# Expert rows loaded and transposed as two half-width tiles in place of two tiles of 128 rows

## Chip, cores and metric

The kernel runs on one core of one Trainium2 chip. The metric is the device time of one execution in microseconds (us), and three executions of the kernel before are given. One further execution was taken with the hardware profiler, and every duration below that comes from a trace is from that one.

## What is computed

The reference does three things in a row, all in float32:

- attention within clusters: 2 batches, 8 heads, 768 positions, head size 64; a query attends to the keys whose nearest of 16 centroids is its own;
- a mixture of 8 experts on the 1536 resulting rows of 512 numbers: every row goes to the one expert that its logits pick;
- a bilinear layer on all rows, 512 to 1536 to 512.

The part that this case is about is the second:

```python
for e in range(E):
    mask = expert_idx == e
    h = np.maximum(x[mask] @ w1[e], 0.0)
    out[mask] = gate_w[mask, None] * (h @ w2[e])
```

## The kernel before

**Rows.** While attention runs, each finished row of `x` is written by an indirect DMA to a table `xs_d` in device memory, in which every expert has a region of its own. An expert's rows therefore lie one behind another, from the start of its region.

**Turns.** The experts are worked off in 8 turns, and the turn of an expert depends on how many rows it has. Turn `e` has a fixed width `WIDTHS[e]`, the number of rows that it takes: 256, 160, 256, 224, 248, 216, 192, 176. Rows that do not fit would go through a rare path (`rare`), which these inputs do not enter. A turn's kind follows from its width: over 224 rows "three", over 176 "two", else "one". The kind says how a float32 product is put together: "three" and "two" use a rounded high part and a low part of both operands (F32R), "one" multiplies plain float32.

**One turn's rows.** `load_xe(e)` reads the expert's first row number from `turn_i` into a register of ScalarE and issues one DMA on ScalarE's queue (line 1194): 256 rows of 2 KB, row `c*128 + p` to partition `p`, tile `c`. It reads 256 rows whatever the width. `trans_x(e)` turns them on TensorE (line 1213): 2 tiles times 4 blocks of 128 columns, eight transposes, the loaded block as weights and the 128x128 identity as the moving operand, into two banks of PSUM. ScalarE and VectorE copy the first `WIDTHS[e]` columns out (lines 1218, 1222, 1224). Turn 0 gets its rows in another way (`near_load`, `near_trans`) and is not touched.

**The order around it.** Loop index `G` counts steps of 128 hidden units, 8 to a turn. A step issues `layer1(G)` (TensorE lines 1232, 1305, 1313, 1314 into `h`, then ScalarE and VectorE make `hh`), at `f == 5` of a turn the transposes for the next turn and the load for the one after, then `layer2(G - 2)` (TensorE lines 1349, 1353, 1354 into `y`), and then `split_some`, which takes weights that were loaded to a ring of four buffers `raw` (DMA on SyncE's queue, line 159), rounds them on ScalarE (line 210) and subtracts on VectorE (line 213); the subtraction frees the buffer for the next load. Each engine works its list off strictly in this order. A step's `h` and the two banks of `trans_x` come from one ring of four PSUM banks (`turn_bank`). `put_rows` writes a turn's result to `ys_d` on SyncE's queue (line 1373). The tile `xe` shares its two buffers with the results `ys`.

Of the kernel before, what the change touches and what calls it, by code (L numbers as in the profile page):

```python
# [9 lines left out]
F32 = mybir.dt.float32  # L10
# [12 lines left out]
P = 128  # L23
FAR = float(2.0 ** 100)
CAP = 256
WIDTHS = (256, 160, 256, 224, 248, 216, 192, 176)
# [25 lines left out]
def kernel(  # L52
# [15 lines left out]
    nc = tc.nc  # L68
# [14 lines left out]
    CT = CAP // P  # L83
# [16 lines left out]
    xs_d = dram.tile([NE * RX, DM], F32, name="xs_d")  # L100
# [157 lines left out]
    identr = left.tile([P, P], F32R, name="identr")  # L258
# [640 lines left out]
    for s in range(nst):  # L899
        g_, h, t = steps[s]  # L900
        pp = g_[0]
        i = s % SPP
# [6 lines left out]
        if s >= SPP and zeros:  # L909
            dst, src = zeros.pop(0)  # L910
# [150 lines left out]
    def new_x(key, dt=F32R):  # L1061
        return big.tile([P, 2, DC, CAP], dt, tag="xT", name=f"xT_{key}", bufs=2)
# [8 lines left out]
    key, cap, held, over, obase, pbase = (left.tile([P, 1, NE], F32, name=n) for n in ("key", "cap", "held", "over", "obase", "pbase"))  # L1071
# [119 lines left out]
    def load_xe(e):  # L1191
        t = big.tile([P, CT, DM], F32R, tag="xe", name=f"xe_{e}", bufs=2)
        at_row = nc.values_load(turn_i[0:1, NE + e:NE + e + 1], engines=[mybir.EngineType.Activation], min_val=RX, max_val=(NE - 1) * RX)
        i = nc.scalar.dma_start(out=t.bitcast(F32), in_=xs_d[bass.ds(at_row, CAP), :].rearrange("(c p) d -> p c d", p=P))
        if e == 1:
            for o in scatters:
                tc.add_manual_dep(i.ins, o.name, DATA, reason="rows of every scatter")
        xe_t[e] = t
# [3 lines left out]
    def turn_bank():  # L1202
        ring[0] += 1
        return ("et0", "et1", "pp", "pv")[(ring[0] - 1) % 4]

    def trans_x(key, src):

        x = new_x(key, F32 if KINDS[key] == "one" else F32R)
        hi, lo = x[:, 0], x[:, 1]
        pts = [ps_t.tile([P, 2, CAP], F32R, tag=turn_bank(), name=f"xT_{key}_{u}") for u in range(2)]  # L1210
        for t in range(CT):
            for j in range(DC):
                nc.tensor.transpose(pts[j // 2][:, j % 2, t * P:(t + 1) * P], src[:, t, j * P:(j + 1) * P], identr)
        pts = [p.bitcast(F32) for p in pts]
        wd = WIDTHS[key]
        if KINDS[key] == "one":
            for u in range(2):
                (nc.vector.tensor_copy if u else nc.scalar.copy)(hi[:, 2 * u:2 * u + 2, :wd], pts[u][:, :, :wd])
            xT_t[key] = x
            return  # L1220
        for u in range(2):
            nc.scalar.copy(hi[:, 2 * u:2 * u + 2, :wd], pts[u][:, :, :wd])
        for u in range(2):
            nc.vector.tensor_sub(lo[:, 2 * u:2 * u + 2, :wd], pts[u][:, :, :wd], hi[:, 2 * u:2 * u + 2, :wd])
        xT_t[key] = x
# [273 lines left out]
    for G in range(total_f + tot + LAG):  # L1499
# [10 lines left out]
        if I < 0:  # L1510
            layer1(G)
            if G in (2, NF - 1):
                load_xe(1 if G == 2 else 2)
            if G == NF:
                further()
            if G == GR - 2:
                tc.mark_branch_hint_location("rare", "LikelyTaken", engines=[mybir.EngineType.DVE])
            e, f = divmod(G, NF)
            if 2 * NF <= G < 3 * NF:
                next(rr, None)  # L1520
            if G > 3 * NF:
                next(gg, None)
            if f == (5 if e else NF - 2):
                if e + 1 < NE:
                    trans_x(e + 1, xe_t[e + 1])
            if f == 5 and 0 < e < NE - 2:
                load_xe(e + 2)
        elif I < tot:
            bil1(I)
            next(pg_, None)  # L1530
# [52 lines left out]
```

## Time and profile before

| | us |
|---|---|
| three executions | 764.43, 764.62, 766.75 |
| median | 764.62 |
| the profiled execution | 765.42 |
| its span in the trace | 763.9 |
| TensorE busy in the span | 750.4 |
| expert turns, by their instructions | about 285 to 460 |

Attention comes first, then the expert turns, then the bilinear layer, whose weights are loaded and split while the last turns run. Trace times are microseconds from the start of the span. PE is TensorE's matrix multiplications, PEld its weight loads, DVE VectorE, ACT ScalarE, POOL GpSimd, SP SyncE; a q behind an engine's name is its queue of DMA issues. "Granted clock" is the share of TensorE's full speed that the chip allowed. A DMA is carried by up to 16 DMA engines; "DMA share" is their mean busy share.

### The profile page before, as it was taken

The numbers are of one execution on the slowest core, as the hardware profiler recorded it, in microseconds if no ns is written. First come the engines' busy times: TensorE is split into PE (matmuls) and PEld (weight loads), VectorE is DVE, ScalarE is ACT, GpSimd is POOL, SyncE is SP. The second block draws the span as 40 slices with busy tenths as digits, with TensorE's granted clock in tenths as the row PEclk, the third lists the DMA queues.
The fourth block names the chain that finished last, engine by engine and source line by source line (L and its number), as shares of the span: only waits on it lengthen the run. The fifth ranks groups of instructions, "written<-read, shape, count | busy, mean of one in ns | idle before, by whom it ended". The sixth has DMA issues, their size and how long they took to land.

```text
span 763.9 us, 12711 instructions
## 1 busy us (share of the span) xinstructions
PE 750.4 (98%) x4788; PEld 629.7 (82%) x4788; DVE 464.3 (61%) x912; ACT 374.3 (49%) x770; POOL 106.3 (14%) x145
## 2 busy tenths in 40 slices
PE   8999999999999999999999999999999999999996
PEld 5767777777777679998999999888898888888995
DVE  6877676787867677478876898677643121121211
ACT  4656766777676675366655565344332121111211
POOL 6303203051300041000000004122001020000201
PEclk9999999999999999999999999999999999999999
DMA  6327133161321026889879877554401010000100
GB/s 189 84 87 252 43 95 90 59 195 58 91 52 32 28 97 231 313 283 298 285 240 279 276 220 219 121 146 111 137 7 52 1 56 0 1 1 0 56 1 28
DMA packets 47747, 91.86 MB, mean 120 GB/s; under 512 B 6264, under 2 KB 19832, under 8 KB 47680
## 3 DMA queue, kind: packets, MB, share of 16 engines
q1 hardware_dynamic: 43472, 81.01, 35.5%
q0 software_dynamic: 2304, 6.31, 2.2%
q10 hardware_dynamic: 1904, 3.67, 1.4%
q8 instruction: 39, 0.64, 0.4%
q14 instruction: 28, 0.23, 0.1%
HBM read 69.27 MB, written 14.04 MB: 109 GB/s over the span
## 4 chain that ended last, share of the span: by engine, by line
issue 28%; PE 26%; DMA 3%; DVE 1%; POOL 1%; ACT 1%; POOLq 0%; SPq 0%; ACTq 0%; DVEq 0%
PE ab L1232 7%; PE y L1349 5%; PE y L1353 3%; PE h L1313 3%; PE h L1232 2%; DMA raw<-in_moe_w_dram 2%; PE h L1305 2%; PE o_sc L1480 1%; PE h L1314 1%; PE y L1354 1%; POOL out_dram L1458 1%; DVE w L213 1%; PE o_pp L1480 1%; PE o_pv L1480 1%; ACT w L210 1%
## 5 line engine op out<-in xcount | busy, mean ns | idle before, releaser
L1436 DVE TENSOR_TENSOR ga<-ab,ga 128x256 f32<-128x256 f32 (+1 forms) x48 | 26.7, 557 | 156.7 <-PE ab L1232 110.9
L634 ACT ACTIVATE E<-sc,nmx 128x768 f32<-128x768 f32 x96 | 86.8, 904 | 53.9 <-DVE nmx L629 46.7
L1232 PE MATMUL ab<-xT_b,w 128*128 128x256 f32 (+1 forms) x720 | 113.1, 304 | 0.0
L1232 PE MATMUL ab<-x,w 128*128 128x512 f32 x432 | 108.1, 390 | 0.0
L1232 PEld LDWEIGHTS ab<-xT_b,w 128*128 128x128 f32 x720 | 98.6, 190 | 7.2
L629 DVE TENSOR_REDUCE nmx<-sc 128x1 f32<-128x768 f32 x96 | 91.4, 953 | 6.8 <-PE sc L621 5.6
L1232 PEld LDWEIGHTS ab<-x,w 128*128 128x128 f32 x432 | 81.1, 188 | 17.2
L652 PEld LDWEIGHTS et<-ident,E 128*128 128x128 f32 x576 | 62.3, 140 | 32.4 <-ACT ET L656 12.8
L1435 ACT COPY ga<-ab 128x256 f32<-128x256 f32 (+1 forms) x48 | 23.1, 481 | 126.9 <-PE ab L1232 123.7
L652 PE MATMUL et<-ident,E 128*128 128x128 f32 x576 | 82.4, 279 | 1.6 <-ACT E L634 1.2
L658 DVE COPY ET<-et 128x384 f32<-128x384 f32 x96 | 52.6, 548 | 50.5 <-PE et L652 50.3
L620 PE MATMUL sc<-K,Q 80*128 80x512 f32 x192 | 73.0, 380 | 0.0
L679 PE MATMUL pv<-ET,v 128*64 128x384 f32 (+2 forms) x408 | 72.3, 479 | 0.3 <-DVE xrow L699 0.2
L213 DVE TENSOR_TENSOR w<-raw,w 128x1024 fp32r<-128x1024 f32 x48 | 58.1, 1218 | 19.3 <-ACT w L210 18.8
L1480 PE MATMUL o_sc<-w,g 128*128 128x512 f32 x288 | 69.5, 390 | 0.0
L1437 ACT CAST g<-ga 128x256 fp32r<-128x256 f32 (+1 forms) x48 | 24.7, 514 | 84.2 <-DVE ga L1436 84.2
L1480 PEld LDWEIGHTS o_sc<-w,g 128*128 128x128 f32 x288 | 53.9, 188 | 11.3
L621 PE MATMUL sc<-K,Q 128*128 128x512 f32 x192 | 61.3, 340 | 0.0
L1349 PE MATMUL y<-hh,w 128*128 128x256 f32 (+3 forms) x416 | 59.2, 290 | 0.0
L210 ACT CAST w<-raw 128x1024 fp32r<-128x1024 f32 x47 | 49.4, 1053 | 16.3 <-DMA raw<-in_moe_w_dram 12.3
L1349 PEld LDWEIGHTS y<-hh,w 128*128 128x128 f32 x416 | 54.4, 190 | 0.3 <-DVE ys L1323 0.3
L656 ACT COPY ET<-et 128x384 f32<-128x384 f32 x96 | 45.7, 476 | 2.7 <-PE et L652 2.7
(277 smaller groups left out, 1206.9 us busy)
## 6 DMA issues: line engine op xcount, KB each, us to landing
raw<-in_moe_w_dram SPq DMA_DIRECT2D x48, 512.0 KB, 5.1
w<-in_moe_w_dram SPq DMA_DIRECT2D x16, 512.0 KB, 9.7
raw<-in_moe_w_a_dram SPq DMA_DIRECT2D x12, 512.0 KB, 5.1
raw<-in_moe_w_b_dram SPq DMA_DIRECT2D x12, 512.0 KB, 4.5
raw<-in_moe_w_out_dram SPq DMA_DIRECT2D x12, 512.0 KB, 3.6
xs_d<-zero SPq DMA_DIRECT2D x8, 512.0 KB, 6.4
xe<-xs_d ACTq DMA_DIRECT2D x7, 512.0 KB, 6.5
v<-in_v_dram SPq DMA_DIRECT2D x8, 384.0 KB, 3.1
```

The source lines that it names most:

```text
L210: (nc.scalar.copy if late is None else nc.vector.tensor_copy)(hi, w)
L213: nc.vector.tensor_sub(lo, w, hi)
L620: nc.tensor.matmul(ps[:, lo:hi], Q3[:, qs], K3[:, h * S + lo:h * S + hi], start=True, stop=False)
L621: nc.tensor.matmul(ps[:, lo:hi], Q2[:, qs], K2[:, h * S + lo:h * S + hi], start=False, stop=True)
L629: nc.vector.tensor_reduce(out=nmx[pp][:, h, t:t + 1], in_=sc[s], axis=AX.X, op=ALU.max, negate=True)
L634: nc.scalar.activation(e, sc.pop(s), AF.Exp, bias=nmx[pp][:, h, t:t + 1], accum_out=sums[pp][:, t, h:h + 1])
L652: nc.tensor.transpose(pt[:, j * P:(j + 1) * P], e[:, kt * P:(kt + 1) * P], ident)
L658: nc.vector.tensor_copy(dst, src)
L679: nc.tensor.matmul(pv[h * D:(h + 1) * D, :], vt[:, h, kt, :], ets[g, h][:, kt, :n * P], start=(kt == 0), stop=(kt == NT - 1))
L1232: nc.tensor.matmul(ps, s_, m_, start=(i == 0), stop=(i == len(ops) - 1))
L1349: nc.tensor.matmul(ys_ps[e][j // 2][:, j % 2, :wd], w[:, m_, ff, j * P:(j + 1) * P], s_, start=(f == 0 and i == 0 and j % 2 == 0), stop=(l ...
L1480: nc.tensor.matmul(o_ps[ck][t], s_[:, t * P:(t + 1) * P], w_[:, m_], start=(f == 0 and i == 0), stop=(J == I and f == NF2 - 1 and i == 2))
```

## The change

For turns 1 to 7 the rows of a turn are loaded as two tiles of `h = WIDTHS[e] // 2` rows: row `c*h + p` goes to partition `p`, tile `c`. The load takes `WIDTHS[e]` rows, not 256, and fills `h` partitions, not 128. The eight transposes take `h` rows each, and the moving operand is the identity's `h` by `h` corner. `h` is 80, 128, 112, 124, 108, 96, 88 for the turns 1 to 7. What is copied out of PSUM is the same columns as before.

```diff
     def load_xe(e):
         t = big.tile([P, CT, DM], F32R, tag="xe", name=f"xe_{e}", bufs=2)
...
-        i = nc.scalar.dma_start(out=t.bitcast(F32), in_=xs_d[bass.ds(at_row, CAP), :].rearrange("(c p) d -> p c d", p=P))
+        h = WIDTHS[e] // CT
+        i = nc.scalar.dma_start(out=t[:h].bitcast(F32), in_=xs_d[bass.ds(at_row, CT * h), :].rearrange("(c p) d -> p c d", p=h))
...
         hi, lo = x[:, 0], x[:, 1]
+        h = WIDTHS[key] // CT
         pts = [ps_t.tile([P, 2, CAP], F32R, tag=turn_bank(), name=f"xT_{key}_{u}") for u in range(2)]
         for t in range(CT):
             for j in range(DC):
-                nc.tensor.transpose(pts[j // 2][:, j % 2, t * P:(t + 1) * P], src[:, t, j * P:(j + 1) * P], identr)
+                nc.tensor.transpose(pts[j // 2][:, j % 2, t * h:(t + 1) * h], src[:h, t, j * P:(j + 1) * P], identr[:h, :h])
```

## Rows read from the trace of the kernel before

**Rows 1.** The page: engine totals, and the granted clock in 40 slices.
```profile
PE 750.4 (98%) x4788; PEld 629.7 (82%) x4788; DVE 464.3 (61%) x912; ACT 374.3 (49%) x770; POOL 106.3 (14%) x145
PEclk9999999999999999999999999999999999999999
```

**Rows 2.** Busy time by stretch in the expert turns; the first line names the columns.
```profile
core 0: us, PE busy (x) PEld busy (x) DVE busy (x) ACT busy (x) POOL busy (x), PEclk, DMA share, GB/s
335.00:350.00 15.00, 13.90 (x120) 13.70 (x118) 12.75 (x24) 9.47 (x16) 0.00 (x0) 1.00 0.90 284
350.00:360.00 10.00, 9.41 (x71) 9.24 (x72) 9.05 (x17) 7.08 (x14) 0.00 (x0) 1.00 0.86 287
360.00:440.00 80.00, 80.00 (x592) 78.69 (x591) 62.12 (x129) 48.06 (x104) 1.26 (x1) 1.00 0.85 269
```

**Rows 3.** TensorE's waits from 285 to 460, the longest: total, times, longest.
```profile
PE h L1232 <- DVE hh L1310: 1.7, 1, 1.7
```

**Rows 4.** The chain that ended last, from 320 to 352: start, length, what.
```profile
319.92 0.69 PE h L1305 x5
...
324.35 7.55 DMA raw<-in_moe_w_dram
...
334.25 5.03 DMA raw<-in_moe_w_dram
...
341.64 6.15 DMA raw<-in_moe_w_dram
```

**Rows 5.** All transposes and loads of the turns' rows: ns min/median/max, first and last start.
```profile
L1213 PE MATMUL xT<-identr,xe x56: 221/247/333, 304.9 to 431.1; 128*128 128x128 f32 x56
L1194 ACTq DMA_DIRECT2D xe<-xs_d x7: 392/392/477, 294.4 to 413.0; - x7
DMA to landing us min/median/max: 5.0/6.5/8.1
```

**Rows 6.** TensorE in order of time, around turn 1's transposes: start, length, what.
```profile
303.74 1.36 PE L1232 MATMUL h<-xT,w 128*128 128x256 f32 x10
304.94 0.80 PE L1213 MATMUL xT<-identr,xe 128*128 128x128 f32 x8
305.57 0.59 PE L1349 MATMUL y<-hh,w 128*128 128x256 f32 x3
```

**Rows 7.** TensorE from 300 to 440: the transposes of turns 3 and 4.
```profile
343.77 0.80 PE L1213 MATMUL xT<-identr,xe 128*128 128x128 f32 x8
...
367.72 0.80 PE L1213 MATMUL xT<-identr,xe 128*128 128x128 f32 x8
```

**Rows 8.** ScalarE from 318 to 440: the issues of the loads for turns 3 and 4.
```profile
324.32 0.48 ACTq L1194 DMA_DIRECT2D xe<-xs_d  x1
...
348.84 0.39 ACTq L1194 DMA_DIRECT2D xe<-xs_d  x1
```

**Rows 9.** DMA from 348.8 to 360: the loads' queue, and the issue with its landing.
```profile
q10 hardware_dynamic: 272, 0.52, 13.6%
...
xe<-xs_d ACTq DMA_DIRECT2D x1, 512.0 KB, 5.3
```

**Rows 10.** The page, the loads' queue: packets, MB, share of 16 engines' span.
```profile
q10 hardware_dynamic: 1904, 3.67, 1.4%
```

**Rows 11.** ScalarE from 352 to 360; in brackets its idle time before, and the releaser.
```profile
355.49 1.05 ACT L210 CAST w<-raw 128x1024 fp32r<-128x1024 f32 x1 [1.73 <-DMA raw<-in_moe_w_dram]
...
358.03 1.05 ACT L210 CAST w<-raw 128x1024 fp32r<-128x1024 f32 x1 [1.01 <-DMA raw<-in_moe_w_dram]
```

**Rows 12.** VectorE from 357 to 361.
```profile
358.13 0.39 DVE L1318 SCALAR_TENSOR_TENSOR hh<-hf,hh 128x224 fp32r<-128x224 f32 x1
...
360.67 0.39 DVE L1318 SCALAR_TENSOR_TENSOR hh<-hf,hh 128x224 fp32r<-128x224 f32 x1
```

**Rows 13.** TensorE from 355 to 364.
```profile
360.20 0.37 PE L1353 MATMUL y<-hh,w 128*128 128x448 f32 x1
...
362.70 0.37 PE L1353 MATMUL y<-hh,w 128*128 128x448 f32 x1
```

## The prediction

> **What bounds the kernel now.** I read the page first. TensorE is busy 750.4 of 763.9 us, and its granted clock stays at the upper level, 2.4 GHz, through all 40 slices [rows 1]. So whatever shortens TensorE's own work is worth its full time, and whatever makes it wait costs its full time, unless a wait elsewhere swallows it. I looked for such waits in the expert turns, where the change lies.
>
> The table of stretches then shows those turns more closely [rows 2]. From 360 to 440 TensorE is busy without a gap. It falls short by 1.10 us between 335 and 350 and by 0.59 us between 350 and 360, and the list of waits names this as one wait of 1.7 us, on VectorE's `hh` [rows 3]. The DMA share is 0.85 to 0.90 in these stretches: the weights stream is close to what the 16 engines carry.
>
> The chain of waits tells what is behind that one wait [rows 4]. It leaves TensorE at about 320.6 and then consists of three loads of raw weights, 7.55, 5.03 and 6.15 us to land, with a rounding on ScalarE and a subtraction on VectorE between them, until `hh` comes late. VectorE and ScalarE work in order, so a late weight load holds up an activation that stands behind it. Two conclusions follow. TensorE time saved between 320 and 350 is lost in that wait, while time saved before 319 or after 351 counts. And the stage has little room for a slower transfer.
>
> **The change, part by part: the transposes.** There are 56, eight a turn [rows 5]. Their time on the path is their pitch, not the 247 ns that one takes: the eight of turn 1 start at 304.94 and the next product at 305.57, so 0.63 / 8 = 79 ns each. The ten products of 256 columns before them take (304.94 - 303.74) / 10 = 120 ns each [rows 6]. The trace shows no such transpose with fewer than 128 columns. From these two rows a column is worth (120 - 79) / 128 = 0.32 ns, and I take that slope, as 128 columns is the nearest width shown and 80 to 124 lies just beyond it. The bounds are no gain at all (the weight load, which still has 128 columns, sets the pitch) and full proportion, 79 / 128 = 0.62 ns a column. The columns saved are 128 - h: 48, 0, 16, 4, 20, 32, 40 for turns 1 to 7. Turn 3's transposes run at 343.8 [rows 7], inside the part whose gain the wait at 350 swallows. That leaves 144 columns times 8 transposes: 1152 x 0.32 = 0.37 us gained, between 0 and 1152 x 0.62 = 0.71. Nothing is removed in number: the same eight weight loads, the same semaphores, the same copies out of PSUM.
>
> **The loads get smaller.** All seven together shrink from 7 x 256 = 1792 to 1472 rows of 2 KB. None is late today: they land after 5.0 to 8.1 us, and the first is issued 304.9 - 294.4 = 10.5 us before its transposes, the last 18 us before [rows 5]. So an earlier landing is worth nothing in itself, and what can count is room for the weights stream beside it. One load takes 13.6% of 16 engines over 11.2 us, which is 1.52 us of every engine, or 95 ns for each of its 16 packets there [rows 9]. Turn 3's load is issued at 324.3, beside the 7.55 us load of the chain [rows 4, 8]. It drops from 16 to 14 packets an engine: 2 x 95 ns = 0.19 us, at most, off the wait at 350. I count 0.18, with 0 to 0.2 as its ends. Turn 1's load shrinks most, 6 x 95 = 0.57 us of every engine, but it runs at 294 [rows 5], before the chain leaves TensorE at 320.6, so I count nothing; if that cover were gone it would be 0.57.
>
> **The loads may get less even.** Today's loads fill 128 partitions and left 1904 packets on their queue, 272 each: 256 of data and 16 more, one for each engine [rows 10]. So each of the 16 engines has had an equal share of 16 rows. 80, 112 and 96 partitions can be cut into 16 equal shares too. 124 (turn 4), 108 (turn 5) and 88 (turn 7) cannot. No row shows what the chip does then. It could give some engines one partition more than others, and nothing would be lost. Or it could keep the shares equal and use fewer engines: 124 = 4 x 31, so 4 engines; 108 = 12 x 9, so 12; 88 = 11 x 8, so 11. Since all seven loads shown have equal shares, I take the second as likelier. Turn 5 would then have 18 packets on 12 engines, 2 x 95 ns more, and turn 7 its old 16 on 11 engines; both are too small to count. Turn 4 would have 62 packets on each of 4 engines, 62 x 95 = 5.9 us of work in place of 1.52: those four engines get 4.4 us more to do.
>
> The Trainium skill speaks on this point, in "DMA: Bandwidth & Descriptors", section "Why a DMA increments its semaphore by 16 and not by 1": the number of engines for one transfer is the largest number up to 16 that divides the slowest dimension of both sides, with 100 partitions on 10 engines as its example. By that rule turn 4 would run on 4 engines and the sum be the one below; without it the first rival's. No run here shows the rule yet, apart from 128 partitions on 16.
>
> **What those 4.4 us cost.** The load itself stays covered: even at half speed beside the weights, 62 packets end about 12 us after the issue at 348.8, near 361, and its transposes are at 367.7 [rows 7, 8]. But every weight load needs all 16 engines to land, so the stream is as late as its slowest four. The engines have 14% idle between 350 and 360 [rows 2], 1.4 us that the four can use to catch up: the stream falls 4.4 - 1.4 = 3.0 us behind. Just there ScalarE already waits for the weights, 1.73 us before the rounding at 355.49 and 1.01 us before that at 358.03 [rows 11], so ScalarE and VectorE take the delay over in full. TensorE does not at once: `hh` is written by 358.52 and first read by `y` at 360.20, the next by 361.06 and read at 362.70 [rows 12, 13], a slack of 1.7 us. TensorE would wait 3.0 - 1.7 = 1.3 us. The ends are 0, if the stream catches up as it goes, and 4.4 - 1.7 = 2.7 if the 14% are gaps that the four engines cannot use. Behind 360 no weight load is waited for that long again and TensorE has no gap until 440, so what is lost there stays lost.
>
> **The sum.** -0.37 (transposes) - 0.18 (chain at 350) + 1.3 (turn 4's load) = +0.75 us. Against the profiled execution's own 765.42 us that is 766.2; the median of the three is 0.80 below the profiled one, so the forecast for the median is 764.62 + 0.75 = 765.4. Its own range, from the ends: -0.71 - 0.2 + 0 = -0.9 to 0 + 0 + 2.7 = +2.7, which is 763.7 to 767.3. A measurement of this kernel can tell about 0.3%, 2.3 us, from no change, so this is no change.
>
> **Rivals.** First, the 124 rows are spread over all 16 engines, or the lag of four is caught up in time. Then only the two gains stand: -0.55, between -0.9 and 0, or 764.1. For it speaks that the load's landing has 6 us to spare and that the stream refills behind 360; against it that ScalarE has no cover at 355 to 358 [rows 11].
>
> Second, and slower: turn 4's load holds back the ring of four `raw` buffers at 350 to 360 by the full 4.4 us, and TensorE finds no slack, because the late activations also hold the PSUM banks that the next `h` needs, earlier than `y` reads them. Then +4.4 - 0.55 = +3.85, or 768.5. It decides against "no change" from a wait of 2.3 + 0.55 = 2.85 us on. For it speaks that the wait at 350 today is of just that kind, an `h` that waits for an `hh` [rows 3]; against it the 1.7 us of slack in the rows that follow.
>
> Third, faster: with less traffic beside it, the chain of three loads lands so much earlier that the wait of 1.68 us at 350 is gone, and the transposes gain in full proportion: -1.68 - 0.71 = -2.4, or 762.2. Against it speaks that only 0.19 us of engine time is taken from beside that chain.
>
> **Chances.** Forecast 0.55, first rival 0.26, second 0.13, third 0.06. The range for 8 in 10 covers the forecast and the first rival with their bounds, and a little for the scatter of the three executions: 763.0 to 767.6. Faster by over 0.3% needs the third rival: 0.06. Slower by over 0.3% needs the second or the forecast's upper end: 0.14. The rest, 0.80, is no change.
>
> **What would show it.** The transposes' pitch in the changed trace: 79 ns at h = 128, 64 ns at h = 80 if the slope of 0.32 holds. Turn 4's load: its time to landing, about 12 us in place of 5.3, and completions on its queue fewer than 16 would show 4 engines. ScalarE's waits for raw weights from 350 to 362: some 3 us more in the forecast, the same as now in the first rival. A new wait of TensorE between 358 and 368, about 1.3 us, shows the forecast's main term; none there shows the first rival; 3 us or more the second. I would be wrong altogether if a difference appeared in attention or in the bilinear layer, where the change touches nothing.

## The result, and the profile after

The changed kernel takes 771.84 us (median of six, 770.92 to 776.44) against 764.52 us for the kernel before on the same chip: a ratio of 1.0098, with an interval of 1.0078 to 1.0118. It is 7.3 us slower, above the end of the forecast's range at 767.6. Its profiled execution took 773.53 us, with a span of 772.0 us, against 765.42 and 763.9 before.

I take the views in the order in which the forecast took them. First the page of the changed kernel: TensorE's total and the queue of the rows' loads (packets, MB, share of the engines' span).

```profile
PE 753.3 (98%) x4788; PEld 631.5 (82%) x4788; DVE 464.6 (60%) x912; ACT 374.4 (48%) x770; POOL 106.2 (14%) x145
...
q10 hardware_dynamic: 1563, 3.02, 1.3%
```

TensorE has as many instructions as before and is busy 2.9 us longer [rows 1], so part of the loss is work that got slower. The queue's packets are 1472 of data, as the change has it, and 91 others, where 16 a load would be 112 [rows 10]. Four loads with 16, and 4, 12 and 11 for turns 4, 5 and 7, make 64 + 27 = 91.

Next, in the changed kernel, TensorE's longest waits from 285 to 470, and the table of stretches around them (columns as in [rows 2]).

```profile
PE y L1355 <- DVE hh L1320: 4.9, 1, 4.9
PE h L1234 <- DVE hh L1312: 1.1, 1, 1.1
```

```profile
core 0: us, PE busy (x) PEld busy (x) DVE busy (x) ACT busy (x) POOL busy (x), PEclk, DMA share, GB/s
...
355.00:360.00 5.00, 5.00 (x39) 4.90 (x38) 2.21 (x3) 0.00 (x0) 0.00 (x0) 1.00 0.96 237
360.00:365.00 5.00, 1.23 (x8) 0.91 (x7) 0.93 (x1) 1.54 (x3) 0.00 (x0) 0.84 0.56 153
365.00:370.00 5.00, 3.83 (x12) 3.34 (x13) 4.13 (x9) 4.56 (x9) 0.00 (x0) 0.50 0.59 196
370.00:375.00 5.00, 5.00 (x33) 4.79 (x32) 4.78 (x12) 3.36 (x7) 0.00 (x0) 0.97 0.80 268
```

The old wait at 350 is still there, a little shorter (1.1 against 1.7 us, [rows 3]). A new one of 4.9 us stands in turn 3's products, where [rows 2] had no gap. From 365 to 370 the granted clock is 0.50, the lower level of 1.2 GHz: TensorE has just waited and now computes at half speed. The DMA share tells the rest: 0.96 from 355 to 360, then 0.56. The engines were nearly all busy first; what a few of them still did afterwards is shown below.

The chain of waits (start, length, what) in the changed kernel names the transfer:

```profile
325.47 8.25 DMA raw<-in_moe_w_dram
...
343.44 5.21 DMA raw<-in_moe_w_dram
...
351.09 11.89 DMA raw<-in_moe_w_dram
363.00 1.05 ACT w L210
...
365.63 0.40 DVE hh L1320
366.17 0.71 PE y L1355
```

A raw weight load takes 11.89 us where its like before had landed by the cast at 355.49 [rows 11]. Rounding, subtraction (left out of the lines above) and `hh` follow it without a gap, and the product starts the moment `hh` is there. ScalarE's order of time has the load's issue and what the weights cost (idle time in brackets):

```profile
349.71 0.53 ACTq L1195 DMA_DIRECT2D xe<-xs_d  x1
...
353.52 1.05 ACT L210 CAST w<-raw 128x1024 fp32r<-128x1024 f32 x1 [0.21 <-DMA raw<-in_moe_w_dram]
...
363.00 1.04 ACT L210 CAST w<-raw 128x1024 fp32r<-128x1024 f32 x1 [8.15 <-DMA raw<-in_moe_w_dram]
...
365.44 1.05 ACT L210 CAST w<-raw 128x1024 fp32r<-128x1024 f32 x1 [0.91 <-DMA raw<-in_moe_w_dram]
```

Turn 4's load is issued at 349.71. In the packet records its data runs from 352.85 to 364.65, so the weight load, issued at 351.09, lands 1.7 us before the uneven load is through. The DMA view from 352.8 to 364.8 has the mean busy share in tenths, in 40 slices of 0.3 us, and the load's queue:

```profile
DMA  3699999895889999987989999999965333222222
...
q10 hardware_dynamic: 252, 0.51, 17.4%
```

From 362.1 on the share is 0.2 to 0.3, where four busy engines of 16 would make 0.25. The weight load's completions, one for each engine, tell the same: twelve came by 356.74, the other four at 360.12, 360.13, 362.96 and 362.97.

Last, TensorE's order of time in the changed kernel: turn 1's transposes, and the products about the wait.

```profile
306.07 0.77 PE L1215 MATMUL xT<-identr,xe 80*128 80x80 f32 x8
306.66 1.70 PE L1351 MATMUL y<-hh,w 128*128 128x256 f32 x12
...
360.97 0.26 PE L1316 MATMUL h<-xT,w 128*128 128x224 f32 x1
366.17 0.71 PE L1355 MATMUL y<-hh,w 128*128 128x448 f32 x1 [4.94 <-DVE hh L1320]
366.68 0.39 PE L1356 MATMUL y<-hh,w 128*128 128x224 f32 x1
...
375.77 0.79 PE L1215 MATMUL xT<-identr,xe 124*128 124x124 f32 x8
```

The starts of each turn's transposes make a ledger of where the time goes (us from the start of the span; the last column is the span):

| | turn 1 | 2 | 3 | 4 | 5 | 6 | 7 | span |
|---|---|---|---|---|---|---|---|---|
| before | 304.94 | 322.50 | 343.77 | 367.72 | 389.56 | 410.97 | 430.51 | 763.9 |
| after | 306.07 | 323.62 | 344.89 | 375.77 | 397.70 | 419.11 | 438.65 | 772.0 |
| later by | 1.13 | 1.12 | 1.12 | 8.05 | 8.14 | 8.14 | 8.14 | 8.1 |

Everything that the change costs comes between turn 3's transposes and turn 4's: 8.05 - 1.12 = 6.93 us. The 1.13 us were there before the first changed instruction: turn 1's load is issued at 295.55, where before it was at 294.42 [rows 5]. In kernels of the experiments that lose no time turn 1's transposes start up to 1.20 us later than before, so I don't count the 1.13 as the change's. The 6.93 consist of three parts. The wait near 350 ends at 351.45 (350.58 before), 0.87 later, which is 0.25 less than turn 3's 1.12. The first product behind the new wait starts at 366.17 (360.20 before, [rows 13]), 5.97 later, so this part adds 5.10. The last is the stretch from there to turn 4's transposes: 375.77 - 366.17 = 9.60 us where before the same work took 367.72 - 360.20 = 7.52, 2.08 us more at the lower clock.

### The profile page after: what moved, and what is told of

Its sections match the earlier page's. It is cut to its first block, busy times and chain, and to the rows that moved or that the text cites. A ratio compares the mean times of both kernels' runs of the same rounds, so it can differ in the third digit from the quotient of the medians.

```text
span 772.0 us, 12709 instructions
## 1 busy us (share of the span) xinstructions
PE 753.3 (98%) x4788; PEld 631.5 (82%) x4788; DVE 464.6 (60%) x912; ACT 374.4 (48%) x770; POOL 106.2 (14%) x145
## 3 DMA queue, kind: packets, MB, share of 16 engines
q10 hardware_dynamic: 1563, 3.02, 1.3%
## 4 chain that ended last, share of the span: by engine, by line
issue 28%; PE 25%; DMA 4%; DVE 2%; POOL 1%; ACT 1%; POOLq 0%; SPq 0%; ACTq 0%; DVEq 0%
PE ab L1234 6%; PE y L1351 4%; DMA raw<-in_moe_w_dram 3%; PE y L1355 3%; PE h L1315 2%; PE h L1234 2%; PE h L1307 2%; PE o_sc L1482 1%; PE y L1356 1%; DVE w L213 1%; PE h L1316 1%; POOL out_dram L1460 1%; PE o_pp L1482 1%; PE o_pv L1482 1%; ACT w L210 1%
```

## The experiments

The theory after the result: turn 4's 124 partitions go to 4 of the 16 DMA engines, the weight loads behind them wait for those four, and TensorE waits for the weights. Rivals: the smaller transposes or the smaller loads themselves, the uneven loads of turns 5 and 7, or the clock as the main cost. Differences of time below are against the kernel before in the same set of runs, whose median was 765.36 us for the first four kernels, 764.13 for the next four and 764.35 for the last four.

**Even loads, all else changed.** The same rows go to the same places, but each load fills all 128 partitions, so that tiles overlap in rows that nothing reads.

```diff
-        i = nc.scalar.dma_start(out=t[:h].bitcast(F32), in_=xs_d[bass.ds(at_row, CT * h), :].rearrange("(c p) d -> p c d", p=h))
+        r = P
+        rows = xs_d[bass.ds(at_row, CAP), :].rearrange("(c p) d -> p c d", p=P)
+        (sp, _), (_, nc_), (sd, nd) = rows.ap
+        rows = dataclasses.replace(rows, ap=((sp, r), (h * sp, nc_), (sd, nd)))
+        i = nc.scalar.dma_start(out=t[:r].bitcast(F32), in_=rows)
...
```

> The changed kernel, but every load of turns 1 to 7 fills all 128 partitions again (row c*h + p to partition p, for p up to 127; partitions h and up hold rows that nobody uses). The transposes stay h rows wide. If the 124-partition load on few DMA engines is the cause: no wait of TensorE over 2 us between 350 and 380, no fall of the granted clock there, and the time back at that of the kernel before, 764.5 within 1.5 us. If the transposes of h rows, or the halves as such, are the cause: the time stays near 771.8.

Measured: 765.04 us, ratio 0.9997 (0.9981 to 1.0013). TensorE's longest waits from 285 to 470, and the stretch in which the changed kernel stood still:

```profile
PE h L1239 <- issue: 0.8, 1, 0.8
PE h L1239 <- DVE hh L1317: 0.4, 1, 0.4
```

```profile
360.00:370.00 10.00, 10.00 (x69) 9.57 (x68) 9.53 (x23) 7.20 (x15) 0.00 (x0) 1.00 0.98 268
```

With even loads the long wait and the low clock are gone, and so is the whole loss. The transposes, which are as in the changed kernel, are free of it, and they bring no gain either.

**Only turn 4 changed.** The other turns are as before; the same edit stands where the transposes set `h`.

```diff
-        h = WIDTHS[e] // CT
+        h = WIDTHS[e] // CT if e == 4 else P
```

> The kernel before, with turn 4 alone (width 248, h = 124) loaded and transposed in the new way. If turn 4's load is the whole cause: about +7 us, 771 to 772.5, with the long wait of TensorE near 361 to 366. If the seven turns share the loss, or code placement does it: well under half of that, 765 to 767.5.

Measured: 771.98 us, ratio 1.0081 (1.0049 to 1.0112). The longest wait, and the stretch:

```profile
PE y L1355 <- DVE hh L1320: 3.7, 1, 3.7
```

```profile
360.00:370.00 10.00, 6.35 (x23) 5.51 (x22) 7.02 (x13) 6.95 (x15) 0.00 (x0) 0.66 0.62 182
```

The change of one turn brings the whole loss, wait and clock included.

**All turns but turn 4 changed.** The same line with `e != 4`.

```diff
-        h = WIDTHS[e] // CT
+        h = WIDTHS[e] // CT if e != 4 else P
```

> The changed kernel, with turn 4 alone loaded and transposed as before. If turn 4's load is the whole cause: 764 to 765, although turns 5 and 7 still load on 12 and 11 DMA engines. If those two cost as well: each of them shows as a later start of the transposes that follow, together over 1 us.

Measured: 765.55 us, ratio 1.0008 (0.9989 to 1.0027), with the wait at 350 as it was and no other of over 0.8 us:

```profile
PE h L1234 <- DVE hh L1312: 1.8, 1, 1.8
```

The loads of turns 5 and 7, on 12 and 11 engines, cost nothing: from turn 4's transposes to turn 7's it takes 62.78 us, and 62.79 before. Together the three runs show the place. What remains is how the 124 partitions turn into 7 us.

**Work in place of the wait.** To ask what the clock costs, a step's `h` products just ahead of the wait are computed four times, 3.8 us more of TensorE work, so that TensorE isn't idle there.

```diff
-            for j in range(DC):
+            for _ in range(4 if G == 26 else 1):
+                for j in range(DC):
...
```

> The changed kernel, in which TensorE computes h of step 26 four times in place of once, with the same result: 24 more matrix products, about 3.8 us of work, placed just ahead of the long wait at 361. If the wait ends with the late weights and costs 4.9 us, and the halved clock behind it costs another 2 us: the extra work fits in the wait, which shrinks to about 1.2 us, the clock stays at the upper level, and the time falls by about 2 us, to 769.5 to 770.5. If the clock falls for another reason or costs nothing: the time stays at 771.8, or rises by up to 3.8.

Measured: 771.78 us (768.16 to 773.11), ratio 1.0079 (1.0056 to 1.0103): the median of the changed kernel, so the gain that was expected didn't come. In its profiled execution, of 768.95 us, ScalarE's wait for the weights is 5.00 us instead of 8.15, TensorE has no long wait behind 360 and the clock stays up:

```profile
358.72 1.05 ACT L210 CAST w<-raw 128x1024 fp32r<-128x1024 f32 x1 [5.00 <-DMA raw<-in_moe_w_dram]
```

```profile
360.00:370.00 10.00, 10.00 (x66) 9.54 (x65) 8.60 (x17) 7.66 (x17) 0.00 (x0) 1.00 0.71 228
```

That execution is one of the two quickest of ten, and here the weights were late by less, so it can't stand for the median. What the run shows is that 3.8 us of extra work cost nothing in the median, as if it fitted into the wait. The clock's own share of the median stays open.

**Loads rounded up to 16 partitions.** As the first experiment, with `r` the next multiple of 16 above `h`; the loads are smaller than before and still even.

```diff
-        r = P
+        r = min(-(-h // 16) * 16, P)
```

> The changed kernel, but each load fills the number of partitions rounded up to a multiple of 16: 80, 128, 112, 128, 112, 96, 96 for turns 1 to 7 (row c*h + p; the partitions past h hold rows nobody uses). Still fewer rows than before. If only the count of DMA engines matters: as the kernel before, 764 to 765.5, perhaps 0.2 us faster by the smaller loads. If a smaller load helps the weights stream beside it by itself: 1 us or more faster.

Measured: 765.06 us, ratio 1.0009 (0.9994 to 1.0023). The queue (1504 packets of data and 7 x 16):

```profile
q10 hardware_dynamic: 1616, 3.08, 1.3%
```

There are 288 fewer data packets than before and no gain can be measured: the traffic that the change saves is worth nothing that shows here.

**Four engines in later turns.** Is it the place or the shape? Turn 4's load is made even, and turns 5, 6 and 7 each fill 124 partitions. The edit is the first experiment's with another `r`.

```diff
-        r = P
+        r = {4: P, 5: 124, 6: 124, 7: 124}.get(e, h)
```

> The changed kernel with turn 4's load over 128 partitions (even), but the loads of turns 5, 6 and 7 over 124 partitions each, so 62 packets on each of 4 engines three times. If a load on four engines costs wherever it is: three times 5 us, 775 to 780. If it costs only where the rounding on ScalarE already waits for weights, as at 350 to 358: under 2 us in all, 764.5 to 766.5.

Measured: 770.92 us, ratio 1.0092 (1.0064 to 1.0121), between the two expectations. By the starts of the transposes the three loads cost 0.09 us (turns 4 to 5), 2.05 (5 to 6) and 3.18 (6 to 7), all different. Another 1.3 us are lost behind turn 7's transposes, where the granted clock is 0.66 from 435 to 440. The two longest waits:

```profile
PE xT L1220 <- DMA xe<-xs_d: 3.0, 1, 3.0
PE y L1360 <- DVE hh L1325: 1.8, 1, 1.8
```

The second is the weights' wait, in turn 5. The first is new: turn 7's transposes wait for their own load. So a load on four engines can also be late itself, and what it costs depends on the place, from nothing to over 4 us.

**Half of the load on four engines.** Turn 4's tile 0 fills 124 partitions and its tile 1 all 128: the four engines carry 31 + 8 = 39 packets, the others 8.

```diff
-            i = nc.scalar.dma_start(out=t[:h].bitcast(F32), in_=xs_d[bass.ds(at_row, CT * h), :].rearrange("(c p) d -> p c d", p=h))
+            nc.scalar.dma_start(out=t[:h, 0].bitcast(F32), in_=xs_d[bass.ds(at_row, h), :])
+            rows = xs_d[bass.ds(at_row, CAP), :].rearrange("(c p) d -> p c d", p=P)[:, 0]
+            i = nc.scalar.dma_start(out=t[:, 1].bitcast(F32), in_=dataclasses.replace(rows, offset=rows.offset + h * DM))
```

> The changed kernel, with turn 4's load as two: tile 0 over 124 partitions (31 packets on each of 4 engines), tile 1 over 128 (8 packets on each of 16). So the four engines carry 39 packets in place of 62. If the delay of the weights goes with the packets beyond an even share (23 in place of 46): half the delay, about 3.3 us, less the slack of 1.7: a wait near 1.6 us, and 766 to 767.5. If any use of four engines is enough: 770 to 772.

Measured: 767.04 us, ratio 1.0034 (1.0019 to 1.0049), as expected of a cost that grows with the packets of the busiest engines, though the wait is half of the 1.6 us expected. The wait and ScalarE's wait for the weights:

```profile
PE y L1361 <- DVE hh L1326: 0.8, 1, 0.8
```

```profile
358.89 1.05 ACT L211 CAST w<-raw 128x1024 fp32r<-128x1024 f32 x1 [4.02 <-DMA raw<-in_moe_w_dram]
```

**Two engines.** The other direction: two loads of 62 partitions, 2 x 31, for turn 4. The queue has 1563 packets again, with 2 + 2 completions in place of 4. The second part's completions come 11 us after the first's, as they would behind it on the same two engines, which then carry 124 packets each.

```diff
-        i = nc.scalar.dma_start(out=t[:h].bitcast(F32), in_=xs_d[bass.ds(at_row, CT * h), :].rearrange("(c p) d -> p c d", p=h))
+        rows = xs_d[bass.ds(at_row, CT * h), :].rearrange("(c p) d -> p c d", p=h)
+        for a, b in (((0, 62), (62, h)) if e == 4 else ((0, h),)):
+            i = nc.scalar.dma_start(out=t[a:b].bitcast(F32), in_=rows[a:b])
```

> The changed kernel, with turn 4's load as two of 62 partitions each, which are 2 x 31: if the engines are the largest number up to 16 that divides the partitions, both run on two engines, with 62 completions in all fewer than sixteen each, and 124 packets on each of those two. The lag then doubles, 108 packets beyond an even share: about 15 us of delay for the weights, a wait of 12 us or more, and the load itself, some 24 us to land, late for its transposes: 780 to 790. If the chip spreads 62 partitions over more engines: 771 or less.

Measured: 770.19 us, ratio 1.0079 (1.0055 to 1.0104): no worse than four engines, against the expectation. ScalarE's waits for the weights are spread over more loads, and TensorE's longest wait is shorter:

```profile
359.12 1.04 ACT L210 CAST w<-raw 128x1024 fp32r<-128x1024 f32 x1 [5.24 <-DMA raw<-in_moe_w_dram]
361.98 1.05 ACT L210 CAST w<-raw 128x1024 fp32r<-128x1024 f32 x1 [1.33 <-DMA raw<-in_moe_w_dram]
365.10 1.05 ACT L210 CAST w<-raw 128x1024 fp32r<-128x1024 f32 x1 [0.61 <-DMA raw<-in_moe_w_dram]
```

```profile
PE y L1357 <- DVE hh L1322: 2.8, 1, 2.8
```

The load drained in 20.8 us, and the weight loads behind it took 9.75, 9.4 and 11.06 us to land. So no weight load waited for the end of this load, and in the changed kernel the first one didn't either (362.97 against 364.65): they are late, but not by the whole of what the uneven load still has to move.

**The changed kernel, a second execution.**

> The changed kernel once more, for a second trace of it. If the long wait is fixed by the packets of turn 4's load: again 4.9 us within 0.3, with the weight load behind it 11.9 us to land. If it hangs on how the two transfers meet: another wait, between 2 and 6 us, since the two other traces with 62 packets on four engines showed 3.7 us, and one that 3.8 us of other work covered.

Measured: 774.77 us in one execution, too few for a verdict on the time. The new wait is 3.1 us, with another of 0.8 behind it and 1.8 at 350, and the granted clock falls twice, to 0.75 from 350 to 355 and to 0.62 from 365 to 370. The weight loads issued while turn 4's load runs, before (350.2 to 356.5) and here (350.5 to 356); the last number is the median time to landing:

```profile
raw<-in_moe_w_dram SPq DMA_DIRECT2D x4, 512.0 KB, 5.1
```

```profile
raw<-in_moe_w_dram SPq DMA_DIRECT2D x3, 512.0 KB, 11.2
```

The median is 6.1 us later; the first weight load behind turn 4's takes 11.53 us, 6.3 more than before, near the 6.6 of the first trace. How the delay splits into waits and slow work differs between executions: from turn 3's transposes to turn 4's it takes 8.9 us more than before here, 6.9 in the first trace.

**Turn 4's load on SyncE's queue**, the one that the weights use, so that the uneven load stands ahead of the weights behind it. The read of its first row number moves to SyncE with it (a line left out below).

```diff
...
-        i = nc.scalar.dma_start(out=t[:h].bitcast(F32), in_=xs_d[bass.ds(at_row, CT * h), :].rearrange("(c p) d -> p c d", p=h))
+        i = (nc.sync if e == 4 else nc.scalar).dma_start(out=t[:h].bitcast(F32), in_=xs_d[bass.ds(at_row, CT * h), :].rearrange("(c p) d -> p c d", p=h))
```

> The changed kernel, with turn 4's load issued on SyncE's queue, the one that the weights use, in place of ScalarE's. The same 62 packets on four engines, but now strictly ahead of the next weight load in one queue. If the excess is the packets alone: the next weight load lands about 4.4 us late, after some 9.7 us, TensorE waits 2 to 3 us, and the time is 767 to 769. If two queues that share four engines make no difference either way: 771 to 772.

Measured: 772.35 us, ratio 1.011 (1.0087 to 1.0134): far from the first expectation and 0.35 us above the second, that the queue makes no difference. The same row, from 350.2 to 356, and the longest wait:

```profile
raw<-in_moe_w_dram SPq DMA_DIRECT2D x4, 512.0 KB, 11.8
```

```profile
PE y L1355 <- ACT ys L1364: 6.4, 1, 6.4
```

With the load ahead of them on their own queue the weights take 11.8 us. From ScalarE's queue the changed kernel's load delays them as much, 11.2 and 11.9 in its two traces. No difference shows here between the two queues.

**Seven and five engines.** Turn 4's load in two parts of 119 = 7 x 17 and 5 partitions: 34 packets on two engines, 36 on five, if the second part uses five of the seven. The edit is against the kernel of the two engines.

```diff
-        for a, b in (((0, 62), (62, h)) if e == 4 else ((0, h),)):
+        for a, b in (((0, 119), (119, h)) if e == 4 else ((0, h),)):
```

> The changed kernel, with turn 4's load as 119 partitions (7 x 17, so 34 packets on each of 7 engines by the largest divisor) and 5 more (2 packets on each of 5). If the delay of the weights grows with the packets beyond 16 an engine: 20 of them in place of 46, under half of the long wait, 766 to 767.5, as with half the load on four engines (767.0). If seven busy engines hold up the weights as four do: 770 to 772.

Measured: 768.44 us (764.99 to 770.04), ratio 1.0058 (1.0039 to 1.0076), between the two expectations. The next weight load takes 8.54 us, and TensorE waits:

```profile
PE y L1357 <- DVE hh L1322: 1.6, 1, 1.6
```

**The same 248 rows in even parts.** 112 and 12 partitions: 16 engines with 14 packets, 12 of them with 2 more. The edit is against the kernel just before.

```diff
-        for a, b in (((0, 119), (119, h)) if e == 4 else ((0, h),)):
+        for a, b in (((0, 112), (112, h)) if e == 4 else ((0, h),)):
```

> The changed kernel, with turn 4's load as two that divide well: 112 partitions (16 engines, 14 packets each) and 12 partitions (12 engines, 2 packets each). The same 248 rows and nothing else. If the share by engine is the cause: no long wait, 764 to 766. If a load of 124 rows costs in itself: 770 or more.

Measured: 765.23 us, ratio 1.0018 (0.9994 to 1.0041), as expected. The queue (completions 16 + 12 in place of 4) and the weight loads from 350.2 to 356:

```profile
q10 hardware_dynamic: 1587, 3.02, 1.4%
```

```profile
raw<-in_moe_w_dram SPq DMA_DIRECT2D x4, 512.0 KB, 5.4
```

The bytes are those of the changed kernel and the time is that of before, so neither the number of rows nor the shape of the transposes is the cause, only how the load is spread over the engines.

The kernel before and all runs in which turn 4's load is changed and not filled up to a multiple of 16, by the packets of its busiest engine. "Next weights": us to landing of the first weight load behind it; "wait": TensorE's longest between 355 and 370; "clock": the lowest granted clock in a stretch of 5 us from 360 to 375.

| turn 4's load | packets | next weights | wait | clock | median, us more |
|---|---|---|---|---|---|
| before, 128 partitions | 16 | 5.3 | none | 1.00 | 0 |
| 112 + 12 | 16 | 6.6 | none | 1.00 | 0.9 |
| 119 + 5 | 36 | 8.5 | 1.6 | 1.00 | 4.1 |
| 124, then 128 | 39 | 7.7 | 0.8 | 1.00 | 2.9 |
| 124 (changed kernel) | 62 | 11.9 | 4.9 | 0.50 | 7.3 |
| the same, second execution | 62 | 11.5 | 3.1 | 0.62 | one execution |
| 124, no other turn changed | 62 | 10.6 | 3.7 | 0.50 | 6.6 |
| 124, with 3.8 us of extra work | 62 | 8.8 | none | 1.00 | 6.4 |
| 124, SyncE's queue | 62 | 11.9 | 6.4 | 0.63 | 8.0 |
| 62 + 62 | 124 | 9.8 | 2.8 | 0.74 | 6.1 |

In these traces the weight load's 16 completions split by the engines that the uneven load uses. With 62 packets on four engines, twelve completions come first and four are late, in all five traces. With 62 + 62 on two engines, fourteen come by 354.67 and two at 357.46 and 359.09; with 119 on seven, nine by 353.14 and seven from 355.19 to 356.49. So the late share is that of the engines with the uneven load. How late it is varies: 8.8 to 11.9 us to landing behind the same 62 packets.

The 0.9 of the second line lies within its interval. None of these kernels beats the kernel before: those that equal it are the ones with even loads.

## Why the prediction was wrong, by its own steps

**The engines: right.** "Turn 4 would have 62 packets on each of 4 engines", 12 for turn 5, 11 for turn 7: the 91 completions are that count, and 1587, 1616, 1571 (119 + 5) and 1563 in the experiments follow from it. This is the rule that the forecast quoted from the Trainium skill, "DMA: Bandwidth & Descriptors", section "Why a DMA increments its semaphore by 16 and not by 1"; the traces agree with it for 124, 119, 108, 88, 62, 12 and 5 partitions, by the completions on the queue. The first rival, an even spread, is out.

**The place, and what is covered: right.** The load took longer than the forecast's 12 us, 15.5 from issue to its last completion at 365.22, but that is still ahead of its transposes, at 367.72 even in the kernel before [rows 7]. The wait came in 358 to 368, on `hh`, behind a late weight load. Turns 5 and 7 cost nothing. What was lost stayed lost: 8.05 us at turn 4, 8.1 at the end.

**The delay of the weights: the step that failed first.** The forecast had "4.4 - 1.4 = 3.0 us behind": 46 packets more than before, at 95 ns [rows 9], less the 14% in which the engines are idle [rows 2]. Measured are 11.89 - 5.27 = 6.6 us. Both terms were wrong. A packet of the load took 135 ns on the four engines, not 95: 17.4% of 16 engines over the 12.0 us of that view, for 248 packets. And the idle share gave nothing back: it is a mean of all 16 engines, and the slices from 352.8 show how such a mean is made up, 0.8 to 0.9 in most of them up to 361.5, then 0.2 to 0.3. With the packets' measured time and no credit the excess would be 62 x 135 - 16 x 95 ns = 6.9 us, an estimate that comes near. The end that the forecast gave, 4.4 us without catching up, was too low for this execution and for two of the other three with the same load on ScalarE's queue, whose delays were 6.3, 5.3 and 3.5 us; so the size isn't fixed by the packets alone.

**The slack: right, and it closes the sum.** The forecast had 1.7 us between a late `hh` and its reader [rows 12, 13]. 6.6 - 1.7 = 4.9, and the wait is 4.94 us. The same sum, delay less 1.7, gives the wait in other traces too: 0.7 us for 124, then 128 (0.8 measured), 1.6 for 119 + 5 (1.6), 2.8 for 62 + 62 (2.8) and 3.6 where only turn 4 is changed (3.7). It misses the second execution (4.6 against 3.1), where the clock had already fallen before and TensorE came later, and SyncE's queue (4.9 against 6.4). The second rival's size of wait (3 us or more) is what appeared, but not for its reason: it needed the slack to be gone, and the slack was there.

**The clock: a term that was missing.** The forecast read a granted clock at the upper level throughout [rows 1] and took a wait to cost its own length. After the wait of 4.94 us the products of 448 columns take 0.60 us and more, 0.37 before [rows 13], until about 370, and the stretch loses another 2.08 us. So the wait costs 4.94 + 2.08 = 7.0 us in that execution. This is from one trace's rows; that the median loses as much through the clock is not shown, since the run that was to tell it didn't.

**The transposes: over-estimated.** Turn 1's eight take 306.66 - 306.07 = 0.59 us at h = 80, against 0.63 at 128 [rows 6]: 74 ns each, not 64. That is 0.04 us for 48 columns, and 144 columns would by that be 0.12 us in place of 0.37 (an estimate). The bound "no gain at all, the weight load sets the pitch" was the nearer one. Their weight loads still have 128 columns and still take 140 ns:

```profile
L1215 PEld LDWEIGHTS xT<-identr,xe x56: 137/140/144, 306.0 to 439.2; 80*128 80x128 f32 x8, 128*128 128x128 f32 x8, 112*128 112x128 f32 x8, 124*128 124x128 f32 x8
```

**"Time saved before 319 counts": not shown.** In the kernel before and the five others whose load of turn 4 is on 128 or 112 + 12 partitions, turn 1's transposes start anywhere from 303.79 to 306.14, and turn 4's only from 367.06 to 367.90: most of a difference at turn 1 is gone by turn 4. The wait at 350 takes up a part of it: it is 1.8 us long behind a start at 304.58, 1.7 behind 304.94 and 0.4 behind 305.81. But it doesn't always: in the kernels with 119 + 5 and with SyncE's queue the transposes start at 303.50 and 303.88, and the wait near 350 is only 0.8 and ends two us earlier than before, ahead of any effect of turn 4's load. These starts differ by more than the gain in question, so no run here tells what a gain at turn 1 is worth.

**The sum as it was and as it is.** Forecast: -0.37 - 0.18 + 1.3 = +0.75. Measured between turns 3 and 4: -0.25 + 5.10 + 2.08 = +6.93, the three parts of the ledger. The sign of the main term and its mechanism were right; the delay was forecast at half of what it was, and the clock came on top.

**What stays open.** Why the weights get so little of the four engines while turn 4's load is there. If an engine took a packet from each queue in turn, the first weight load, 16 packets an engine, would lose 16 x 95 ns = 1.5 us; it loses 6.6, and when it lands at 362.97, 209 of the load's 248 packets have started, 52 an engine beside its own 16. The Trainium skill, "DMA: Bandwidth & Descriptors", section "Queues, rings and completion order", has each engine alternate between the queues a packet at a time, where such a packet typically holds 9 to 17 descriptors. No view here shows how many of the profile's packets make up one of those, so the order can't be worked out from these traces. Open is also why the delay varies between executions, from 3.5 to 6.6 us for the same load, and why two engines with 124 packets each aren't worse than four with 62.

## What to carry to other kernels

Before a load's partition count is cut to what is needed, look at how it divides: 124 partitions went to 4 engines and cost 7 us, and the same rows as 112 + 12, or with the partitions filled up to 128, cost nothing that can be measured. Price such a load by the stream that shares its engines: the delay of that stream, less the slack of the place, was the wait here. As a first estimate of the delay take the whole of the busiest engine's packets, without any credit for the engines' mean idle share: at 95 ns each that is 3.4, 3.7 and 5.9 us for 36, 39 and 62 packets, where 3.3, 2.4 and 3.5 to 6.6 were measured. For 124 packets on two engines it is far too high, 11.8 against 4.5. And where TensorE is the bound and its clock is at the upper level, a wait of several microseconds has a second cost in the slower work behind it.

## What the runs showed of the hardware that was not expected

- A load on another queue can delay the weights as much as one on their own: 11.2 and 11.9 us to landing in the changed kernel's two traces against 11.8, and 5.1 with an even load.
- Only the engines that carry the uneven load are late for the weights: two, four or seven of 16 completions, with the uneven load on two, four or seven engines.
- The delay is not in proportion to the busiest engine's packets: 5.3, 8.5, 7.7 and 9.8 us to landing for 16, 36, 39 and 124, and 8.8 to 11.9 for 62.
- The granted clock fell behind waits of 2.8, 3.0, 3.1, 3.7, 4.9 and 6.4 us (0.74, 0.66, 0.62, 0.50, 0.50 and 0.63 in the lowest stretch of 5 us) and stayed at 1.00 behind those of 0.8 and 1.6 us in turn 3 and of 1.8 us in turn 5. But in the second execution of the changed kernel it was 0.75 already around a wait of 1.8 us at 350, where the kernel before had a wait of 1.7 at 1.00 [rows 2, 3], so the length of one wait doesn't decide alone.
- A transpose's pitch hardly follows its moving columns: 74 ns at 80 and 79 at 128.
